# One-bank PSUM tiles after attention, GpSimd scaling of three blocks, and uneven row groups in an attention and feed-forward kernel

## The chip, the cores and the metric

The kernel runs on one core of one Trainium2 chip. The metric is the device time of one execution in microseconds (us); of several executions the median counts. Five engines of the core run their own instruction lists in order and wait for each other by semaphores: TensorE (PE, with its weight loads as PEld), VectorE (DVE), ScalarE (ACT), GpSimd (POOL) and SyncE (SP), which here issues nearly all DMA transfers.

## What is computed

Attention of 4 batches, 8 heads, 768 positions and head width 64, in which a query sees the 8 first keys and its 96 last ones, with a bias that falls with the distance; then a feed-forward layer of width 2048 with a sigmoid gate on the 3072 resulting rows:

```python
scores = scale * q @ k.T + bias                  # per batch and head
scores = where(is_global | is_local, scores, -1e9)
a = exp(scores - max(scores)); a = a / (sum(a) + 1e-09)
x = (a @ v) as 3072 rows of 512
h = x @ w_in                                     # 512 -> 2048
out = (h / (1 + exp(-h))) @ w_out                # 2048 -> 512
```

## The kernel before

**Blocks.** Attention is done in 24 blocks of 128 rows. For a block, PE turns K and Q into the layout it needs (`turn`, L626, copied out by ACT at L634) and multiplies them (`scores`, L659) into the four-bank PSUM tile `four`. DVE adds the bias and finds the maxima (`top_of`, L669, eight instructions), ACT takes the exponentials with their sums (`expo`, L677, eight instructions of 128x136), DVE inverts the sums (`guard`, `inverse`, L681 and L685), ACT multiplies by them (`norm`, L689, eight instructions), DVE transposes the result in two halves (`turn_p`, L703), and PE multiplies it with V (`values`, L722), into `four` again. `x_high` (ACT, L731) and `x_low` (DVE, L734) split the block's result into two parts for the first layer. GpSimd does small copies: the keys that a block shares with the one before (`carry`, L648 and L650) and the columns of the 8 first keys (`aside`, L694).

**First layer.** Blocks are collected in groups of row tiles (`GS`, eight groups of three). For each group and each of 16 slices f of w_in, `moe_h` (L819) issues 12 matmuls, which take the group's rows as columns (3 x 128 = 384), into one bank. ACT takes a tanh from it (L825), DVE multiplies (L829), and a DMA puts the result into DRAM (`moe_put`, L834). w_in arrives as raw 64-bit numbers, 1 MB at a time (`ws`, L431), and is turned into two float parts by three DVE instructions (L439, L445, L451), an ACT cast (L457) and a DVE subtraction (L461).

**Second layer.** Rows are taken in 12 pairs of row tiles. Each pair needs seven products (`product`, L876) of 24 matmuls with 256 columns, from sums and differences of quarters that are read back from DRAM. For a product ACT casts (`split_hi`, L866) and DVE subtracts (`split_lo`, L870); for some, DVE first adds quarters (`sums`, L856). Three buffers hold split inputs (`hl`). Each product is summed in one PSUM bank. It is then evicted by ACT (`keep_half`, L890) or DVE (`add_half`, L893) into the output tile. Beside that, DVE checks the number formats of all weights (L552, L558) and of V (L606), and at the end gathers the verdict (L1014 to L1081), by which a branch decides on a general version.

**Banks.** There are eight PSUM banks: four tiles of one bank each (`bank0` to `bank3`) and `four`, which is one tile of four banks. In the second layer a product takes any free bank of the eight; banks 4 to 7 are slices of `four`:

```python
four = psum.tile([P, 4, 512], F32, name="four")
banks = [psum.tile([P, 512], F32, name=f"bank{i}") for i in range(4)] + [four[:, i] for i in range(4)]
```

**Order.** A planner (`Plan.run`) goes through all operations with assumed costs and latencies and ranks from the table `PAR`, and writes each engine's list in the order in which it would have started them. Where its PE has nothing to do before the first layer, it puts in a matmul without use (`filler`, L1103). The recording layer derives waits from which tiles an instruction reads and writes.

Of the kernel before, what the change touches and what calls it, by code (L numbers as in the profile page):

```python
# [10 lines left out]
F32 = mybir.dt.float32  # L11
# [8 lines left out]
PSUM = bass.MemoryType.PSUM  # L20

P = 128
# [3 lines left out]
NR = 4  # L26
CH = Q + 2
WIN = NR * CH
# [9 lines left out]
    CAP=dict(po=6, h=4, tp=2), CST=dict(t=480, s=1000, top=220, exp=395, sc=300, tp=597, o=1500, o0=800, g=330),  # L38

    C0=17.5, CR=1.05, LW=14, LB=5.5, QB=3.5, RN=-1.8, RP=1.4, RV=2.0, RB=1.5, VL=1.5, SP=0, TE='ACT', KS=66, KE=203, KD=10000.0, KV=14990,  # L40

    BP=(4, 2), CF=8, AHEAD=9, GS=(3,) * 8, BD=(1, 0), EQ=4, B1R=-0.5, Q1=450, Q2=2400, CD=9, CS=3, SQ=((0, 0, 8), (1, 0, 8)), PB=4, AQ=4, O0=10.0, ON=11, PF=23,
# [147 lines left out]
def attn_moe(ctx, tc, q, k, v, n_global, n_local, w_in, w_out, out):  # L190
# [43 lines left out]
    four = psum.tile([P, 4, 512], F32, name="four")  # L234
# [166 lines left out]
    o_bias = steps(bias_own, [70, 200, 597, 597, 597], -4, [o, o_far], [*bt, tb])  # L401
    o_bias1 = steps(bias_prev, [570, 80, 80], PAR['B1R'], [o_bias], bt)
    o_b = {}
    for a in range(2):
        for first in (True, False):
            dve = bias_eng(first, a) is nc.vector
            o_b[first, a] = op(
                "DVE" if dve else "ACT", 597 if dve else 560, 2 * a - 0.5 if first else PAR["RB"] + 2 * a,
                (lambda first=first, a=a: bias_of(first, a)), [o_bias if first else o_bias1], bt,
            )  # L410
# [105 lines left out]
    def open_late():  # L516
        attn.close()
        st["late"] = ctx.enter_context(tc.tile_pool(name="late", bufs=1))
# [168 lines left out]
    def norm(i, a, c):  # L687
        x, m = blk[i]["p", a][:, c], a * NR + c
        nc.scalar.mul(x, x, blk[i]["S"][:, m:m + 1])  # L689
# [54 lines left out]
    for i in range(B * NJ):  # L744
# [43 lines left out]
        for n in ((0, 1),) if not PAR["SP"] else ((0,), (1,)):  # L788
# [4 lines left out]
            for a in n:  # L793
                o_y = [op("ACT", CST["sc"], r, (lambda i=i, a=a, c=c: norm(i, a, c)), [o], [pes_[a]]) for c in range(NR)]
                if j:
                    o_f.append(op("POOL", 150, r, (lambda i=i, a=a: aside(i, a)), o_y + o_n[-2:-1], [pes_[a], gs]))
                o_t.append(op("DVE", CST["tp"], r, (lambda i=i, a=a: turn_p(i, a)), o_y, [pes_[a], pts[a]]))
# [134 lines left out]
    for g in range(NPAIR):  # L932
# [9 lines left out]
        for m, (src, c) in enumerate(PROD):  # L942
# [19 lines left out]
            for p in range(HF):  # L962
                o = op("PE", 355, r, (lambda g=g, m=m, p=p, po=po: product(g, m, p, po)),
                       [hi, lo, *o_w2[p], o], [hl, po])
                if not g and not m and not p:
                    o["hold"] = 2
            o_p.append(o)
# [315 lines left out]
```

## Time and profile before

| | us |
|---|---|
| median of 3 runs | 669.76 (668.48 to 670.19) |
| the profiled execution | 672.28 |
| its span, first to last instruction | 670.5 |
| mean granted TensorE clock | 0.993 |
| busy: PE, DVE, ACT, POOL | 641.5, 514.6, 351.0, 32.7 |

The profile is of one execution, which took 2.5 us more than the median. Busy times are sums over the span; matmuls overlap, so the spacing of their starts says more than their durations. "Idle before" at a row is the time in which the engine waited just ahead of it, with the instruction that ended the wait; "issue" stands for idle time that no wait explains.

### The profile page before, as it was taken

The numbers are of one execution on the slowest core, as the hardware profiler recorded it, in microseconds if no ns is written. First come the engines' busy times: TensorE is split into PE (matmuls) and PEld (weight loads), VectorE is DVE, ScalarE is ACT, GpSimd is POOL, SyncE is SP. The second block draws the span as 40 slices with busy tenths as digits, with TensorE's granted clock in tenths as the row PEclk, the third lists the DMA queues.
The fourth block names the chain that finished last, engine by engine and source line by source line (L and its number), as shares of the span: only waits on it lengthen the run. The fifth ranks groups of instructions, "written<-read, shape, count | busy, mean of one in ns | idle before, by whom it ended". The sixth has DMA issues, their size and how long they took to land. (4 is left out here: it accounts for less than half of the span.)

```text
span 670.5 us, 20175 instructions
## 1 busy us (share of the span) xinstructions
PE 641.5 (96%) x8308; PEld 608.5 (91%) x8308; DVE 514.6 (77%) x1132; ACT 351.0 (52%) x915; POOL 32.7 (5%) x127
## 2 busy tenths in 40 slices
PE   8979989999999999999999999999999999999996
PEld 6859879999999999999999998988998999999996
DVE  5777886868845445467457989988998889999995
ACT  5958872598648556579454433333333333333431
POOL 4111100001000000010000000000000000000000
PEclk9989999999999999999999999999999999999999
DMA  7974997647645456653546788576658556656321
GB/s 123 232 218 109 289 225 223 183 119 192 167 113 124 109 145 165 167 137 82 136 115 205 239 237 282 189 224 215 198 161 255 180 181 190 208 191 218 106 80 35
DMA packets 180372, 116.83 MB, mean 174 GB/s; under 512 B 105396, under 2 KB 162996, under 8 KB 180276
## 3 DMA queue, kind: packets, MB, share of 16 engines
q1 hardware_dynamic: 179602, 115.24, 61.5%
q8 instruction: 66, 1.08, 0.7%
q10 hardware_dynamic: 674, 0.26, 0.1%
q14 instruction: 30, 0.25, 0.1%
HBM read 84.02 MB, written 31.46 MB: 172 GB/s over the span
## 5 line engine op out<-in xcount | busy, mean ns | idle before, releaser
L819 PE MATMUL bank<-xh,wi 128*128 128x384 f32 x1024 | 279.2, 344 | 0.0
L819 PEld LDWEIGHTS bank<-xh,wi 128*128 128x128 f32 x1024 | 187.7, 189 | 6.0 <-issue 5.3
L819 PE MATMUL bank<-xl,wi 128*128 128x384 f32 x512 | 173.2, 338 | 0.0
L876 PE MATMUL four<-wo,g 128*128 128x256 f32 x1035 | 133.1, 284 | 13.2 <-DVE o L893 9.8
L876 PEld LDWEIGHTS four<-wo,g 128*128 128x128 f32 x1035 | 125.8, 189 | 18.3 <-DVE o L893 13.5
L829 DVE SCALAR_TENSOR_TENSOR th<-th,bank 128x384 f32<-128x384 f32 x128 | 70.6, 552 | 69.2 <-ACT th L825 66.4
L825 ACT ACTIVATE th<-bank 128x384 f32<-128x384 f32 x128 | 62.6, 489 | 103.2 <-PE bank L819 101.8
L876 PE MATMUL bank<-wo,g 128*128 128x256 f32 x945 | 116.2, 282 | 0.0
L876 PEld LDWEIGHTS bank<-wo,g 128*128 128x128 f32 x945 | 113.8, 189 | 0.0
L819 PEld LDWEIGHTS bank<-xl,wi 128*128 128x128 f32 x512 | 97.0, 189 | 0.0
L866 ACT CAST g<-S 128x1024 fp32r<-128x1024 f32 x48 | 50.0, 1049 | 66.3 <-DVE S L856 34.9
L677 ACT ACTIVATE pe<-pe,NM 128x136 f32<-128x136 f32 x192 | 75.9, 399 | 5.9 <-DVE NM L669 5.8
L689 ACT ACTIVATE pe<-pe,S 128x136 f32<-128x136 f32 x192 | 61.8, 399 | 2.4 <-DVE S L685 2.4
L870 DVE TENSOR_TENSOR g<-S,g 128x1024 fp32r<-128x1024 f32 x48 | 58.4, 1219 | 2.3 <-ACT g L866 2.1
L866 ACT CAST g<-a 128x1024 fp32r<-128x1024 f32 x36 | 37.7, 1048 | 41.7 <-PE four L876 21.7
L669 DVE CUSTOM_DVE_ANT_0 pe<-four,B 128x136 f32<-128x136 f32 x192 | 45.2, 292 | 14.1 <-PE four L659 12.6
L870 DVE TENSOR_TENSOR g<-a,g 128x1024 fp32r<-128x1024 f32 x36 | 43.9, 1220 | 2.6 <-ACT g L866 2.5
L558 DVE TENSOR_REDUCE TOP<-c 128x1 f32<-128x512 int16 x64 | 43.0, 678 | 1.0 <-DMA c<-in_moe_w_in_dram 1.0
L703 DVE STREAM_TRANSPOSE pt<-pe 128x512 f32<-128x512 f32 x48 | 34.0, 708 | 12.3 <-ACT pe L689 12.2
L722 PEld LDWEIGHTS four<-pt,vt 32*64 32x64 f32 x2496 | 33.3, 130 | 5.8 <-issue 5.0
L677 ACT ACTIVATION_READ_ACCUMULATOR pe<-pe,NM 128x1 f32 x192 | 36.6, 191 | 0.0
L722 PE MATMUL four<-pt,vt 32*64 32x96 f32 (+3 forms) x2496 | 36.0, 243 | 0.0
(128 smaller groups left out, 575.2 us busy)
## 6 DMA issues: line engine op xcount, KB each, us to landing
gate<-th SPq DMA_DIRECT2D x128, 192.0 KB
a<-gate SPq DMA_DIRECT2D x48, 512.0 KB
ws<-in_moe_w_in_dram SPq DMA_DIRECT2D x8, 1024.0 KB
w<-in_moe_w_out_dram SPq DMA_DIRECT2D x16, 512.0 KB
c<-in_moe_w_in_dram SPq DMA_DIRECT2D x16, 512.0 KB
c<-in_moe_w_out_dram SPq DMA_DIRECT2D x16, 512.0 KB
vt<-in_v_dram SPq DMA_DIRECT2D x64, 96.0 KB
va<-in_v_dram SPq DMA_DIRECT2D x24, 256.0 KB
```

Source lines behind the costliest of these rows:

```text
L558: nc.vector.tensor_reduce(TOP[:, i, n:n + 1], top, AX.X, (ALU.min, ALU.max)[i], apply_absolute_value=True)
L669: nc.vector.tensor_tensor_reduce(blk[i]["p", a][:, c], four[:, c // 2 * 2 + a, c % 2 * WIN:(c % 2 + 1) * WIN], (B1 if i % NJ else B0)[:, a ...
L677: nc.scalar.activation(x, x, AF.Exp, bias=NM[:, n:n + 1], scale=-1.0, accum_out=blk[i]["S"][:, m:m + 1])
L689: nc.scalar.mul(x, x, blk[i]["S"][:, m:m + 1])
L703: nc.vector.transpose(y[:, :NR * NR * Q].rearrange("p (a r q) -> p a r q", a=NR, q=Q), x[:, :, :, :Q])
L722: nc.tensor.matmul(o, x, y, start=w == line[0], stop=w == line[-1])
L819: nc.tensor.matmul(ph, w1[f // 2][:, w, c, f % 2 * P:(f % 2 + 1) * P], x[:, c, :SIZE[g] * P], start=not c and not n, stop=c == NCC - 1 and ...
L825: nc.scalar.activation(th, mo["ph", g, f], AF.Tanh, scale=0.5)
L829: nc.vector.scalar_tensor_tensor(gf, gf, 1.0, mo["ph", g, f], ALU.add, ALU.mult)
L866: nc.scalar.copy(x[:, 0], mo["a", g, PROD[m][0]])
L870: nc.vector.tensor_sub(x[:, 1], mo["a", g, PROD[m][0]], x[:, 0].bitcast(F32))
L876: nc.tensor.matmul(y, a[:, i, p], w2[p, w, c], start=not p and not n, stop=p == HF - 1 and n == 2,)
```

## The change

When attention has ended (`open_late`), the four-bank tile is given back, and four one-bank tiles take its place, so that every product of the second layer lies in a tile of its own. The first matmul of the second layer is now put behind that point. For the first three blocks (`NB=3`) GpSimd multiplies by the inverted sums, in two instructions of 128x544 for a block instead of eight on ACT. The sums are inverted for each half by itself (`SP=1`). The first layer's groups have 3, 3, 2, 4, 4, 4, 4 row tiles. Some twenty numbers of the planner's table differ.

```diff
-    C0=17.5, CR=1.05, LW=14, LB=5.5, QB=3.5, ..., SP=0, TE='ACT', KS=66, KE=203, ...
+    C0=19.2, CR=1.35, LW=15, LB=3, QB=4.5, ..., SP=1, TE='ACT', NB=3, KS=64, KE=187, ...
-    BP=(4, 2), CF=8, AHEAD=9, GS=(3,) * 8, BD=(1, 0), ...
+    BP=(4, 2), CF=8, AHEAD=27, GS=(3, 3, 2, 4, 4, 4, 4), BD=(2, 1), ...
...
-    four = psum.tile([P, 4, 512], F32, name="four")
+    early = ExitStack()
+    ctx.enter_context(early)
+    four = early.enter_context(tc.tile_pool(name="four", bufs=1, space=PSUM)).tile([P, 4, 512], F32, name="four")
...
     def open_late():
         attn.close()
+        early.close()
+        x = ctx.enter_context(tc.tile_pool(name="last", bufs=1, space=PSUM))
+        banks[4:] = [x.tile([P, 512], F32, name=f"bank{i}") for i in range(4, 8)]
...
     def norm(i, a, c):
-        x, m = blk[i]["p", a][:, c], a * NR + c
-        nc.scalar.mul(x, x, blk[i]["S"][:, m:m + 1])
+        if c is None:
+            x = blk[i]["p", a]
+            y = blk[i]["S"][:, a * NR:(a + 1) * NR].unsqueeze(2).to_broadcast([P, NR, WIN])
+            nc.gpsimd.tensor_mul(x, x, y)
+        else:
+            x, m = blk[i]["p", a][:, c], a * NR + c
+            nc.scalar.mul(x, x, blk[i]["S"][:, m:m + 1])
...
+                if i < PAR["NB"]:
+                    o_y = [op("POOL", CST["scp"], r, (lambda i=i, a=a: norm(i, a, None)), [o], [pes_[a]])]
...
                     o["hold"] = 2
+                    plan.after(o, o_late)
```

PE in the second layer before, where a product in `four` ends and the next one in `four` begins (g is the split input, wo the weights, and the wait names the engine whose semaphore is waited for):

```order
L876 MATMUL four<-wo_0_6289,g_5_7332 128x256
L876 MATMUL four<-wo_1998,g_6_7371 128x256 [waits Activation_49]
L876 MATMUL four<-wo_1998,g_6_7371 128x256
L876 MATMUL four<-wo_1998,g_6_7371 128x256 [waits DVE_49]
L876 MATMUL four<-wo_2656,g_6_7371 128x256 x3
L876 MATMUL four<-wo_2977,g_6_7371 128x256 [waits DVE_49]
L876 MATMUL four<-wo_2977,g_6_7371 128x256 x2
```

The same place after:

```order
L889 MATMUL bank_5565<-wo_1984,g_6_7350 128x256 [waits Activation_49]
L889 MATMUL bank_5565<-wo_1984,g_6_7350 128x256
L889 MATMUL bank_5565<-wo_1984,g_6_7350 128x256 [waits DVE_49]
L889 MATMUL bank_5565<-wo_2264,g_6_7350 128x256 x3
L889 MATMUL bank_5565<-wo_2906,g_6_7350 128x256 x3
```

The first two waits, for the two parts of the split input, are in both; the third, for a DVE eviction that reads another bank of `four`, is gone. Before, 26 matmuls of the second layer wait for a DVE eviction and 9 for an ACT eviction of the tile `four`; after, none does.

ACT before, around the scaling of blocks 1 and 2 (pe is a half of a block's scores):

```order
L689 ACTIVATE pe_79<-pe_79,S 128x136 x4
L689 ACTIVATE pe_80<-pe_80,S 128x136 x4
L677 ACTIVATE pe_77,S<-pe_77,NM 128x136 x3
L634 COPY QT<-bank_91 128x512
L677 ACTIVATE pe_78,S<-pe_78,NM 128x136 x4
L731 CAST xh<-four 128x4x128
L457 CAST wi_704<-ws_465 128x1024
L689 ACTIVATE pe_77<-pe_77,S 128x136 x4
L689 ACTIVATE pe_78<-pe_78,S 128x136 x4
```

POOL after, for the same two blocks:

```order
L696 TENSOR_TENSOR pe_79<-pe_79,S 128x544
L704 COPY pgr_104<-pe_79 128x4x8
L655 COPY KT<-KT 128x4x4x2
L653 COPY KT<-KT 128x4x102
L696 TENSOR_TENSOR pe_80<-pe_80,S 128x544
L704 COPY pgr_104<-pe_80 128x4x8
L655 COPY KT<-KT 128x4x4x2
L653 COPY KT<-KT 128x4x102
L696 TENSOR_TENSOR pe_77<-pe_77,S 128x544
L704 COPY pgr_103<-pe_77 128x4x8
L696 TENSOR_TENSOR pe_78<-pe_78,S 128x544
```

The sixteen scalings of these blocks left ACT's list, and four multiplications entered POOL's, between the copies of keys that the next block's scores wait for. On PE, 200 fillers became 173: ahead of the first matmul of the first layer there stand 191 before and 173 after.

SP before, where the loads of K and Q for later blocks (kn, qn), the last raw w_in parts (ws), V (vt) and stores of the first layer (gate) stand in a row:

```order
L431 DMA ws_1462<-in_moe_w_in_dram 128x4x512
L834 DMA gate_1033<-th 384x1x128
L587 DMA kn<-in_k_dram 128x8x64
L587 DMA qn<-in_q_dram 128x8x64
L594 DMA vt<-in_v_dram 32x12x64 x8
L834 DMA gate_1033<-th 384x1x128
L587 DMA kn<-in_k_dram 128x8x64
L834 DMA gate_1712<-th 384x1x128
L431 DMA ws_1721<-in_moe_w_in_dram 128x4x512
```

SP after, there:

```order
L592 DMA kn<-in_k_dram 128x8x64
L592 DMA qn<-in_q_dram 128x8x64
L847 DMA gate_1070<-th 384x1x128
L599 DMA vt<-in_v_dram 32x12x64 x8
L847 DMA gate_1070<-th 384x1x128
L433 DMA ws_1617<-in_moe_w_in_dram 128x4x512
L433 DMA ws_1679<-in_moe_w_in_dram 128x4x512
L847 DMA gate_1710<-th 384x1x128 x2
L592 DMA kn<-in_k_dram 128x8x64
```

One pair of K and Q moved ahead of the last two ws loads, and the K load behind V now stands behind both of them.

## Rows read from the trace of the kernel before

**Rows 1.** Busy time by stage (core: us, engines busy (x instructions), PEclk, DMA share, GB/s)

```profile
0.00:50.20 50.20, 42.94 (x884) 34.80 (x885) 32.33 (x115) 35.04 (x118) 11.95 (x54) 0.97 0.87 191
50.20:405.10 354.90, 351.53 (x5400) 332.42 (x5399) 245.00 (x699) 223.12 (x691) 20.80 (x73) 1.00 0.63 166
405.10:665.70 260.60, 246.82 (x2026) 241.16 (x2024) 236.37 (x319) 92.88 (x107) 0.00 (x0) 1.00 0.58 184
```

**Rows 2.** Waits of PE in the second layer: us in total, times, longest

```profile
PE four L876 <- DVE o L893: 9.8, 18, 1.0
PE four L876 <- ACT E L890: 1.4, 3, 0.5
PE four L876 <- ACT o L890: 1.4, 3, 0.5
```

**Rows 3.** Timeline of PE in the second layer: start, us, instruction, xcount [idle before]

```profile
418.81 8.35 PE L876 MATMUL bank<-wo,g 128*128 128x256 f32 x69
...
437.28 1.67 PE L876 MATMUL four<-wo,g 128*128 128x256 f32 x12 [0.52 <-DVE o L893]
439.47 1.33 PE L876 MATMUL four<-wo,g 128*128 128x256 f32 x9 [0.52 <-DVE o L893]
...
501.69 5.86 PE L876 MATMUL bank<-wo,g 128*128 128x256 f32 x48
```

**Rows 4.** Waits of DVE in the second layer

```profile
DVE o L893 <- PE four L876: 14.2, 22, 1.1
DVE g L870 <- ACT g L866: 4.7, 11, 0.7
...
DVE o L893 <- PE bank L876: 1.6, 4, 0.6
DVE TOP L558 <- DMA c<-in_moe_w_in_dram: 1.0, 2, 0.7
```

**Rows 5.** Timeline of DVE around the fifth product of a pair

```profile
501.89 0.42 DVE L893 SCALAR_TENSOR_TENSOR o<-four,o 128x256 f32<-128x256 f32 x1 [0.79 <-PE four L876]
502.24 1.22 DVE L870 TENSOR_TENSOR g<-S,g 128x1024 fp32r<-128x1024 f32 x1
503.37 0.42 DVE L893 SCALAR_TENSOR_TENSOR o<-bank,o 128x256 f32<-128x256 f32 x1
```

**Rows 6.** Timeline of PE at the end of the first layer

```profile
403.96 0.51 PE L819 MATMUL bank<-xh,wi 128*128 128x384 f32 x2
...
404.48 0.51 PE L819 MATMUL bank<-xh,wi 128*128 128x384 f32 x2
```

**Rows 7.** Timeline of PE ahead of the first layer: fillers, and scores with their stops

```profile
31.32 2.14 PE L1103 MATMUL bank<-wx 128*128 128x256 bf16 x18
...
36.63 1.16 PE L659 MATMUL four<-KT,QT 64*32 64x136 f32 x32 [2.55 <-issue]
...
48.92 0.53 PE L659 MATMUL four<-KT,QT 64*32 64x136 f32 x17 [1.83 <-issue]
...
50.27 0.67 PE L819 MATMUL bank<-xh,wi 128*128 128x384 f32 x1
```

**Rows 8.** Timeline of ACT, POOL and DVE ahead of the first layer

```profile
32.88 2.50 ACT L689 ACTIVATE pe<-pe,S 128x136 f32<-128x136 f32 x8
...
40.87 0.52 POOL L648 COPY KT<-KT 128x408 f32<-128x408 f32 x1 [2.67 <-DVE NM L669]
...
46.82 1.22 DVE L445 SCALAR_TENSOR_TENSOR ws<-ws 128x1024 uint32<-128x1024 uint32 x1
...
47.55 0.56 POOL L694 COPY pgr<-pe 128x32 f32<-128x32 f32 x1 [6.15 <-ACT pe L689]
48.81 0.21 POOL L694 COPY pgr<-pe 128x32 f32<-128x32 f32 x1 [0.70 <-ACT pe L689]
```

**Rows 9.** Timeline of PE where K and Q are waited for

```profile
86.19 0.63 PE L626 MATMUL bank<-ident,kn 128*128 128x128 f32 x4 [1.86 <-DMA kn<-in_k_dram]
...
88.63 0.63 PE L626 MATMUL bank<-ident,qn 128*128 128x128 f32 x4 [0.76 <-DMA qn<-in_q_dram]
```

More of the change, by code (lines that the diff above doesn't have):

```diff
@@ L36 @@
     LAT=140, SD=125, DL=2100, DV=2300, DW=2900, DB=3500, DS=3500, DO=3400, MG=60, T2=45000, LAT2=230, MG2=400, F0=600, F1=1200, C1=400, C2=1650, COLD=4400, WEND=60000,
-    CAP=dict(po=6, h=4, tp=2), CST=dict(t=480, s=1000, top=220, exp=395, sc=300, tp=597, o=1500, o0=800, g=330),
-    C0=17.5, CR=1.05, LW=14, LB=5.5, QB=3.5, RN=-1.8, RP=1.4, RV=2.0, RB=1.5, VL=1.5, SP=0, TE='ACT', KS=66, KE=203, KD=10000.0, KV=14990,
-    BP=(4, 2), CF=8, AHEAD=9, GS=(3,) * 8, BD=(1, 0), EQ=4, B1R=-0.5, Q1=450, Q2=2400, CD=9, CS=3, SQ=((0, 0, 8), (1, 0, 8)), PB=4, AQ=4, O0=10.0, ON=11, PF=23,
+    CAP=dict(po=6, h=4, tp=2), CST=dict(t=435, s=1220, top=220, exp=393, sc=300, scp=1150, tp=610, o=1880, o0=1050, g=330),
+    C0=19.2, CR=1.35, LW=15, LB=3, QB=4.5, RN=3, RP=-0.4, RV=2.4, RB=8.5, VL=0.0, SP=1, TE='ACT', NB=3, KS=64, KE=187, KD=10000.0, KV=11530,
+    BP=(4, 2), CF=8, AHEAD=27, GS=(3, 3, 2, 4, 4, 4, 4), BD=(2, 1), EQ=4, B1R=-4.0, Q1=450, Q2=2400, CD=9, CS=3, SQ=((0, 0, 8), (1, 0, 8)), PB=4, AQ=4, O0=5.0, ON=15.0, PF=24,
 )
@@ L400, in attn_moe @@
     o = op("PE", 120, -99, (lambda tp=tb: spread_par(tp)), [o], [tb])
-    o_bias = steps(bias_own, [70, 200, 597, 597, 597], -4, [o, o_far], [*bt, tb])
-    o_bias1 = steps(bias_prev, [570, 80, 80], PAR['B1R'], [o_bias], bt)
+    o_bias = steps(bias_own, [190, 300, 762, 821, 821], -4, [o, o_far], [*bt, tb])
+    o_bias1 = steps(bias_prev, [701, 273, 550], PAR['B1R'], [o_bias], bt)
     o_b = {}
@@ L407, in attn_moe @@
             o_b[first, a] = op(
-                "DVE" if dve else "ACT", 597 if dve else 560, 2 * a - 0.5 if first else PAR["RB"] + 2 * a,
+                "DVE" if dve else "ACT", 530 if dve else 646, 2 * a - 0.5 if first else PAR["RB"] + 2 * a,
                 (lambda first=first, a=a: bias_of(first, a)), [o_bias if first else o_bias1], bt,
@@ L793, in attn_moe @@
             for a in n:
-                o_y = [op("ACT", CST["sc"], r, (lambda i=i, a=a, c=c: norm(i, a, c)), [o], [pes_[a]]) for c in range(NR)]
+                if i < PAR["NB"]:
+                    o_y = [op("POOL", CST["scp"], r, (lambda i=i, a=a: norm(i, a, None)), [o], [pes_[a]])]
+                else:
+                    o_y = [op("ACT", CST["sc"], r, (lambda i=i, a=a, c=c: norm(i, a, c)), [o], [pes_[a]]) for c in range(NR)]
                 if j:
```

## Prediction

> **What bounds the kernel now.** I read the busy times by stage first [rows 1]. They cut the span at the first matmul of the first layer (50.2 us), at the first of the second layer (405.1) and at its last (665.7). In the middle stage PE is busy for 351.5 of 354.9 us, so nothing but PE's own work sets its length. In the last stage PE is busy for 246.8 of 260.6 us and DVE for 236.4: both are close to being the bound. In the first stage no engine is full (PE 42.9, ACT 35.0, DVE 32.3 of 50.2 us); there a chain of waits sets the time, and a good part of PE's work is fillers.
>
> Next come the waits of PE in the second layer [rows 2]: 18 times for a DVE eviction (9.8 us) and 6 times for an ACT one (2.8 us), always for a product that was about to be computed in another bank of `four`. The idle time of 0.52 us is not the whole price of such a stop, and the timeline shows what is [rows 3]. In a run without stops, 69 matmuls start within 8.07 us (8.35 less the last one's 0.28), which is 0.1187 us from start to start. The run of 12 that begins at 437.28 starts its last matmul at 438.67, and the next begins at 439.47: 0.80 us instead of 0.12, and the first matmuls behind a stop are slower too (9 take 1.33 us, without a stop it would be 8 x 0.1187 + 0.28 = 1.23). So a stop costs about 0.8 us. From the other side: 2016 matmuls by 0.1187 are 239.3 us, the stage took 260.6, so 21.3 us are lost; some 0.7 of it is the few matmuls of the checks, and the rest over 25 stops (the 24 of the rows, and one of the kind at the end for the verdict) is 0.8 us again.
>
> **The change, part by part.** *One-bank tiles.* The lists show that none of the second layer's matmuls waits for an eviction of its neighbour's bank any more. That takes 24 stops by 0.8 us, 19.2 us, off PE. What is late next is DVE. It has 236.4 us of work in that stage [rows 1], and the change takes only a last piece of weight preparation out of it (0.7 us), against 239.3 us of PE. Its waits are of two kinds [rows 4]. It waits 15.8 us for products that it is to evict: that is DVE being ahead, and this shrinks as PE gets faster. It waits 4.7 us for ACT casts and 1.0 us for transfers, and these may stay. How much room there is shows at the fifth product of a pair, the tightest one [rows 5]: DVE waits 0.79 us for a product to end, evicts it from 501.89, subtracts from 502.24 and is done at 503.46. PE runs on without a stop [rows 3]: its product begins 24 matmuls after 501.69, at 504.54, and needs the subtracted part with its third matmul, at 504.78. That is 1.3 us of slack, and for these five products DVE kept pace with an unstopped PE. A pair takes PE 168 x 0.1187 = 19.9 us, and DVE on average 236 / 12 = 19.7. A pair with more checks than average, or a late ACT cast, therefore eats the slack. I allow 2 us for stops of that new kind (floor 0, and up to 9 by the rival below): 19.2 - 2 = 17.2 us gained.
>
> *Uneven row groups.* Three matmuls of 384 columns take 0.52 us [rows 6], 0.1735 each; one of 256 columns takes 0.1187 [rows 3]. The line through both gives 0.2283 for 512 columns. 1536 x 0.1735 = 266.5 us become 384 x 0.1735 + 768 x 0.2283 + 192 x 0.1187 = 264.7: a gain of 1.8 us. No row shows 512 columns; in proportion to the columns (0.2313) the gain would be -0.5, and the line's is nearer, since it is drawn through two rows. I take 1.5. The ACT and DVE work of the wider pieces is the same number of elements in fewer instructions, and in the middle stage it lies under PE (ACT 223, DVE 245 of 355 us).
>
> *GpSimd scaling and the start.* ACT loses 24 instructions ahead of the first layer; eight take 2.50 us [rows 8], so 7.5 us of its 35.0. The last block of a chain then no longer waits for eight scalings but for one GpSimd multiplication of its half. None is in the trace: a copy of 408 elements takes 0.52 us there [rows 8], so 544 elements with one input would be 0.70, and twice that, 1.4, with two inputs; I take 1.2, nearer to the upper one since both operands are read. Six of them cost GpSimd 7.2 us of a stage in which it idles for 38. What waits behind them there are the key copies for the next block's scores; since the multiplications are released by other blocks' exponentials, I cost that at nothing, and if the cover is gone at 1.2 us for each of three blocks. What PE gets of all this is read from its list: 27 fillers fewer at 0.109 us ((2.14 - 0.28) / 17 [rows 7]), 2.9 us. PE stops twice on scores for 2.55 and 1.83 us without a wait that the profile shows [rows 7]; I leave them as they are, as the same loads are queued around them. If they vanished as well, the stage would be 4.4 us shorter; if the shorter list only means longer stops, nothing is gained.
>
> *Loads.* Behind 50 us, PE waited 1.86 and 0.76 us for K and Q [rows 9], while weights were loading. In the new list one K and Q pair goes ahead of the last two weight parts, the next one behind both. I expect one place relieved and one made worse: 0, with 3 us to the good (all those waits) and 4 to the bad (a megabyte more to pass before K).
>
> *The end.* The verdict's last instructions move behind the last product on DVE: 0.5 us lost (0 to 2).
>
> *Sum.* 672.3 (the profiled execution: 670.5 of span and 1.8 around it) - 17.2 - 1.5 - 2.9 - 0 + 0.5 = 651.2 us. That execution is 2.5 us above the median of the runs, 669.76, so for a median I say 648.7.
>
> **A rule against the change.** A small GpSimd copy took 0.56 us at 47.55, and 0.21 at 48.81 [rows 8]; the long one ended just when a DVE instruction with two inputs in SBUF did (46.82 + 1.22 = 48.04). The Trainium skill, SBUF - State Buffer, section Who interferes with whom, says that such a DVE instruction and a GpSimd one that reads SBUF exclude each other for the whole instruction; the trace agrees for the copy. The Trainium skill, GPSIMD Engine Reference, section 3.1, measures 4497 ns for a two-input operation of 2048 elements, by which an estimate for 544 is 1.2 us; no run here shows it. By that figure the sum would be the same.
>
> **The rivals.** *DVE takes PE's place in the second layer.* If DVE's waits for ACT and transfers stay (5.7 us) and half of those for products do (7.9), the stage lasts 235.7 + 13.6 = 249.3 us, a gain of 11.3 instead of 17.2: 654.6. For it: DVE's 236 us against 239. Against it: the slack of 1.3 us that comes back in each pair.
>
> *GpSimd and DVE hold each other up.* The six multiplications fall among DVE's two-input weight instructions of 1.2 us each. If each holds DVE, or is held, for its whole time, that is 7.2 us in a stage in which DVE idles for 18; with half of it on the chain, the start loses 3.6 and the 2.9 is not gained: 655.2. That is the rule of the SBUF page above, at its price by the rows.
>
> *Everything falls well.* PE at its floor in the second layer (2.0 more), the two stops at the start gone (4.4), K and Q in time (2.6): 639.7.
>
> *K and Q late for all that follows: slower.* The table's shorter lead for loads (`LB` from 5.5 to 3) could leave each block waiting as at 86 us, 2.6 us for a block. From nine of the some 18 blocks after the first layer's start on, that eats the 21 us; at 12 blocks it gives 648.7 + 31.2 = 680. Against it: PE is idle for only 3.4 us of the whole middle stage [rows 1], of which the two waits at 86 and 88 us are 2.6, and DMA there has a mean share of 0.63, so that loads have room later on.
>
> *It does not do what it says.* If stops of the same size come back at the same places, because the evictions are needed for another reason, what is left is 669.8 - 3.9 = 665.9. The waits are gone from the list, so this is unlikely.
>
> **How the numbers follow.** Forecast 0.55; DVE as the bound 0.22; GpSimd and DVE 0.07; everything well 0.09; K and Q late 0.04; no effect on the stops 0.03. The forecast's own spread is 644 to 653. The range reaches to the two rivals at 655 and partly to the one at 640: 642 to 657. Faster than before by over 0.3%, about what a measurement of this kernel can tell from no change, is every case but the late loads: 0.95; slower 0.04; the same 0.01.
>
> **What would show it.** In the profile after, the waits of PE for L893 and L890 of before must be gone in the second layer; if PE then waits for the subtraction (L870), above all at a pair's fifth product, DVE is the bound, and the stage is near 249 us instead of 243. The first layer's 512-column matmuls should be 0.228 us apart. The first of them all should come at about 47 us. A GpSimd multiplication far above 1.4 us, or DVE instructions of 2 us beside it, would show the rival at the start. The prediction is wrong if the second layer is not at least 10 us shorter, or if the middle stage is longer than before.

## The result, and the profile after

The changed kernel takes 650.8 us (median of 4 runs, 645.2 to 653.7) against 670.0 for the kernel before in the same session: a ratio of 0.970, with a 95% interval of 0.9625 to 0.978. The forecast was 648.7, with a range of 642 to 657. A second set of runs gave 651.0 (645.3 to 653.0), ratio 0.9727 (0.9702 to 0.9752). The profiled execution of after took 653.09 us, 2.3 more than the median; its span is 651.3. By stage (start, first layer, second layer, tail; columns as in [rows 1]):

```profile
0.00:49.20 49.20, 40.97 (x863) 32.88 (x864) 35.39 (x129) 27.13 (x92) 19.03 (x60) 0.97 0.86 195
49.20:407.37 358.17, 350.77 (x5204) 296.50 (x5203) 245.66 (x721) 218.55 (x674) 22.09 (x73) 1.00 0.63 165
407.37:647.46 240.09, 240.09 (x2025) 239.87 (x2023) 233.12 (x315) 92.83 (x107) 0.00 (x0) 1.00 0.62 199
647.46:651.30 3.84, 0.31 (x5) 0.10 (x4) 0.96 (x3) 0.00 (x0) 0.00 (x0) 1.00 0.15 47
```

Against [rows 1] the second layer is 20.5 us shorter (260.6 to 240.1), the start 1.0 and the tail 1.0 (4.8 to 3.8), and the stage of the first layer is 3.3 us longer. That is the 19.2 us between the two profiled executions, and the second layer alone is more than all of it.

In the second layer PE is busy for 240.09 of 240.09 us. None of the waits of [rows 2] is left, nor any other, and the first run there is unbroken over six products, with (17.83 - 0.28) / 147 = 0.1194 us from start to start:

```profile
407.37 17.83 PE L889 MATMUL bank<-wo,g 128*128 128x256 f32 x148
```

DVE is what changed places with it. Its waits there, which answer to [rows 4]:

```profile
DVE o L906 <- PE bank L889: 2.7, 5, 1.0
DVE g L883 <- ACT g L879: 2.5, 4, 1.5
```

It waited 15.8 us for products before and 2.7 now, 4.7 us for casts before and 2.5 now: most of the 24 us in which DVE was idle before was time in which it was ahead of a stopped PE. 7 us are left.

The start and the first layer went less well. Every row of PE's timeline with an idle time of over 1 us between 2 us and the end of the first layer:

```profile
35.58 0.45 PE L664 MATMUL four<-KT,QT 64*32 64x136 f32 x11 [3.42 <-issue]
48.96 0.49 PE L631 MATMUL bank<-ident,qn 128*128 128x128 f32 x3 [2.32 <-issue]
72.08 0.66 PE L631 MATMUL bank<-ident,kn 128*128 128x128 f32 x4 [1.30 <-DMA kn<-in_k_dram]
79.86 0.69 PE L631 MATMUL bank<-ident,kn 128*128 128x128 f32 x4 [1.04 <-DMA kn<-in_k_dram]
...
96.30 0.63 PE L631 MATMUL bank<-ident,kn 128*128 128x128 f32 x4 [1.24 <-DMA kn<-in_k_dram]
...
161.36 0.39 PE L832 MATMUL bank<-xl,wi 128*128 128x256 f32 x1 [1.88 <-issue]
...
184.01 0.63 PE L631 MATMUL bank<-ident,qn 128*128 128x128 f32 x4 [1.51 <-DMA qn<-in_q_dram]
```

The four waits for K and Q come to 5.1 us. The two stops on the way to the first layer, which answer to [rows 7], grew from 4.4 to 5.7 us. And the matmuls of 512 columns, in the first layer's last groups:

```profile
371.90 0.39 PE L832 MATMUL bank<-xl,wi 128*128 128x512 f32 x1
372.13 0.63 PE L832 MATMUL bank<-xh,wi 128*128 128x512 f32 x2
372.60 0.40 PE L832 MATMUL bank<-xl,wi 128*128 128x512 f32 x1
```

Three of them take 0.70 us, 0.2333 each, against 0.1735 for 384 columns [rows 6].

### The profile page after: what moved, and what is told of

It reads as the page before. It is cut to its first block, busy times and chain, and to the rows that moved or that the text cites. A ratio compares the mean times of both kernels' runs of the same rounds, so it can differ in the third digit from the quotient of the medians.

```text
span 651.3 us, 19662 instructions
## 1 busy us (share of the span) xinstructions
PE 632.1 (97%) x8089; PEld 569.3 (87%) x8089; DVE 515.1 (79%) x1166; ACT 338.5 (52%) x873; POOL 41.1 (6%) x133
## 5 line engine op out<-in xcount | busy, mean ns | idle before, releaser
L832 PE MATMUL bank<-xh,wi 128*128 128x512 f32 (+2 forms) x896 | 264.0, 368 | 0.0
L889 PE MATMUL bank<-wo,g 128*128 128x256 f32 x1980 | 237.2, 281 | 0.0
L889 PEld LDWEIGHTS bank<-wo,g 128*128 128x128 f32 x1980 | 235.9, 189 | 0.2
L832 PEld LDWEIGHTS bank<-xh,wi 128*128 128x128 f32 x896 | 163.2, 188 | 28.0 <-issue 5.4
L832 PE MATMUL bank<-xl,wi 128*128 128x512 f32 (+2 forms) x448 | 162.3, 362 | 1.9 <-issue 1.9
L842 DVE SCALAR_TENSOR_TENSOR th<-th,bank 128x512 f32<-128x512 f32 (+2 forms) x112 | 68.0, 608 | 69.8 <-ACT th L838 69.1
L838 ACT ACTIVATE th<-bank 128x512 f32<-128x512 f32 (+2 forms) x112 | 60.0, 535 | 112.9 <-PE bank L832 109.9
L832 PEld LDWEIGHTS bank<-xl,wi 128*128 128x128 f32 x448 | 84.2, 188 | 12.6 <-issue 2.3
L674 DVE CUSTOM_DVE_ANT_0 pe<-four,B 128x136 f32<-128x136 f32 x192 | 46.1, 291 | 18.3 <-PE four L664 18.0
L664 PE MATMUL four<-KT,QT 64*32 64x136 f32 x1536 | 29.4, 280 | 3.7 <-issue 3.4
L664 PEld LDWEIGHTS four<-KT,QT 64*32 64x32 f32 x1536 | 22.1, 105 | 10.7 <-issue 9.2
```

The lines of the kernel that those rows point to most:

```text
L664: nc.tensor.matmul(o, t["QT"][r, g, Q * c:Q * (c + 1)], t["KT"][r, g, c:c + NR], start=True, stop=True)
L674: nc.vector.tensor_tensor_reduce(blk[i]["p", a][:, c], four[:, c // 2 * 2 + a, c % 2 * WIN:(c % 2 + 1) * WIN], (B1 if i % NJ else B0)[:, a ...
L832: nc.tensor.matmul(ph, w1[f // 2][:, w, c, f % 2 * P:(f % 2 + 1) * P], x[:, c, :SIZE[g] * P], start=not c and not n, stop=c == NCC - 1 and ...
L838: nc.scalar.activation(th, mo["ph", g, f], AF.Tanh, scale=0.5)
L842: nc.vector.scalar_tensor_tensor(gf, gf, 1.0, mo["ph", g, f], ALU.add, ALU.mult)
L889: nc.tensor.matmul(y, a[:, i, p], w2[p, w, c], start=not p and not n, stop=p == HF - 1 and n == 2,)
```

## The experiments

Each kernel was timed beside the kernel before, on the same chip as that. They did not all run on one chip, so small differences between kernels are read from the ratios. "First" is the start of the first layer, "layer 1" and "layer 2" the lengths of the two stages in the kernel's profiled execution, as they are cut above.

| kernel | median us | ratio to before (95%) | first | layer 1 | layer 2 |
|---|---|---|---|---|---|
| before | 669.5 to 670.0 | | 50.2 | 354.9 | 260.6 |
| after | 650.8 | 0.9702 (0.9625 to 0.9780) | 49.2 | 358.2 | 240.1 |
| after, again | 651.0 | 0.9727 (0.9702 to 0.9752) | 42.8 | 356.7 | 240.1 |
| four_kept | 675.0 | 1.0055 (1.0027 to 1.0084) | 49.6 | 357.5 | 263.6 |
| split_only | 651.8 | 0.9733 (0.9689 to 0.9778) | 49.5 | 352.0 | 242.4 |
| dve_more12 | 659.6 | 0.9850 (0.9804 to 0.9896) | 43.1 | 356.4 | 249.5 |
| shift64 | 650.5 | 0.9707 (0.9662 to 0.9752) | 46.1 | 357.0 | 241.6 |
| long_fillers | 648.9 | 0.9693 (0.9663 to 0.9724) | 43.0 | 357.0 | 240.1 |
| split_scale | 652.6 | 0.9728 (0.9699 to 0.9757) | 48.1 | 353.4 | 246.2 |
| act_scales | 648.2 | 0.9665 (0.9642 to 0.9688) | 47.0 | 356.9 | 240.2 |
| groups_of_3 | 656.2 | 0.9794 (0.9772 to 0.9817) | 47.7 | 356.1 | 243.9 |
| early_loads | 652.9 | 0.9730 (0.9706 to 0.9753) | 48.2 | 358.3 | 241.4 |
| gp_3to5 | 647.7 | 0.9683 (0.9652 to 0.9714) | 46.7 | 353.7 | 241.3 |
| gp_3to8 | 646.3 | 0.9655 (0.9629 to 0.9681) | 46.3 | 354.8 | 240.1 |

### Is it the tile? four_kept and split_only

```diff
 # four_kept: the kernel after
     def open_late():
         attn.close()
-        early.close()
-        x = ctx.enter_context(tc.tile_pool(name="last", bufs=1, space=PSUM))
-        banks[4:] = [x.tile([P, 512], F32, name=f"bank{i}") for i in range(4, 8)]
```

> The kernel after with one part undone: the four-bank tile stays to the end, so the products of the second layer lie in its slices again. All orders are those of after. If the tile was the cause of the stops, they come back, some 24 to 26 of about 0.8 us, the second layer takes 259 to 262 us instead of 240, and the time is 651 + 20 = 671 us (667 to 675). Rival: the second layer became shorter because the table's new numbers ordered its DVE and ACT work better; then the stage stays under 250 us and the time under 661.

It took 675.0 us, 24 more than after and even 0.55% more than before. The stops are back, and the shape is that of [rows 2] and [rows 3]:

```profile
407.10:670.70 263.60, 247.71 (x2025) 241.32 (x2023) 236.08 (x316) 92.94 (x107) 0.00 (x0) 1.00 0.55 181
```

```profile
PE four L886 <- DVE o L903: 10.4, 20, 0.6
PE four L886 <- ACT E L900: 2.4, 5, 0.5
PE four L886 <- ACT o L900: 1.9, 4, 0.5
PE four L886 <- DVE CS L1022: 0.9, 1, 0.9
PE four L886 <- DVE RV L1033: 0.3, 1, 0.3
```

29 stops behind evictions instead of 24, two more behind weight checks, and a stage 23.5 us longer than after's: 0.76 us for each of the 31, or 0.81 if the evictions' 29 are made to pay for all of it. The prediction had 0.8 from before's rows.

```diff
 # split_only: the kernel before, with the edit above put in, and
                     o["hold"] = 2
+                    plan.after(o, o_late)
```

> The kernel before with this part alone: one-bank tiles when attention ends, and the first product put behind that point. Everything else, its table and its groups, is as before. If the tile is the whole cause, the second layer falls from 260.6 to 240 us and the time from 670 to about 649.5 (647 to 653). Rival: DVE, which has 236.4 us of work there, becomes the bound: the stage is near 249 us with PE waiting for the subtraction (L870 of before) and the time near 658.

651.8 us: this part by itself gives 17.7 us, about as much as the whole change. The second layer lasts 242.4 us, and PE waits only twice:

```profile
PE bank L1014 <- DMA c<-in_moe_w_out_dram: 0.9, 1, 0.9
PE bank L881 <- DVE g L875: 0.8, 1, 0.8
```

One is for the load of a weight check and one for a subtraction. The rival of 249 us is out. What else was changed is worth about 1 us in all, within the spread of the runs; that this is a sum of gains and losses is seen below.

### How near is DVE? dve_more12

```diff
 # the kernel after, in split_lo
         nc.vector.tensor_sub(x[:, 1], mo["a", g, PROD[m][0]], x[:, 0].bitcast(F32))
+        if m == 0:
+            nc.vector.tensor_sub(x[:, 1], mo["a", g, PROD[m][0]], x[:, 0].bitcast(F32))
```

> The kernel after, with the subtraction of the first product of each of the 12 pairs written twice, so DVE has 12 x 1.14 = 13.6 us more to do in the second layer; nothing else differs. DVE was busy for 233.1 of 240.1 us there, so 7 us were free. If DVE is close behind PE, as the prediction's second case has it, the free 7 us are used up and the stage lasts 233.1 + 13.6 = 246.7 us and up to 4 more for waits that stay: 247 to 251, and the time is 658 to 662. Rival: DVE's place in time leaves no use for the free time, since each doubled instruction stands right ahead of a product that waits for it; then each pair loses close to the whole 1.14 us, the stage lasts 253 to 254 and the time is about 664. If PE does not feel it, 651.

```profile
399.53:649.04 249.51, 243.55 (x2025) 240.47 (x2023) 244.62 (x326) 91.56 (x107) 0.00 (x0) 1.00 0.59 192
```

```profile
PE bank L891 <- DVE g L883: 5.0, 7, 1.2
PE bank L891 <- DVE g L885: 0.8, 2, 0.6
```

The first of the 12 repeats ran ahead of the stage, at 371 us, so DVE has 11.5 us more to do in it (busy for 244.6 instead of 233.1). Of these 9.4 come out as time (240.1 to 249.5), and only 2.1 fit into the 7 us in which DVE was idle. Seven of the nine stops (5.0 of 5.8 us) are not behind the repeated subtraction but 98 matmuls into a pair, at the third matmul of its fifth product, as in these rows:

```profile
564.17 11.79 PE L891 MATMUL bank<-wo,g 128*128 128x256 f32 x98
577.11 8.19 PE L891 MATMUL bank<-wo,g 128*128 128x256 f32 x67 [1.16 <-DVE g L883]
```

That is the place that the prediction named as the tightest. So it is DVE's work as a whole that holds PE up, and not only that a longer instruction stands right ahead of a product: DVE is then the bound, as in the prediction's second case. That case was near, with some 1% of DVE's work (2.1 of 233 us) between it and the forecast, but it was not the case of this kernel. The profiled execution was the fastest of the four, 4.9 us under their median.

### What are PE's stops at the start? after again, shift64 and long_fillers

In the trace of after, 64 transfers on a queue of kind "instruction" go with 8089 weight loads and as many matmuls of PE, 253 of them a piece.

```profile
PE 632.1 (97%) x8089; PEld 569.3 (87%) x8089; DVE 515.1 (79%) x1166; ACT 338.5 (52%) x873; POOL 41.1 (6%) x133
...
q8 instruction: 64, 1.05, 0.7%
```

The two stops at the start come at the 613th and the 870th record of PE's weight loads, the few waits between the loads counted as records too (without them, the 606th and the 862nd load; where a text here says "613th load", the record is meant). The two places are about twice 128 records apart. The records of the queue show a packet of 16 KB from 32.99 to 34.30 us, 1.28 us ahead of the restart at 35.58, and one from 46.44 to 47.40, 1.56 us ahead of the restart at 48.96. In before the stops of [rows 7] lie at the 614th and 870th record, with packets that end at 35.17 and 47.43 us, 1.46 and 1.49 us ahead of the restarts. One of the packets, by the queues' sums in the stretch from 32.95 to 34.35 us of after:

```profile
q1 hardware_dynamic: 499, 0.29, 104.7%
q8 instruction: 1, 0.02, 5.8%
```

The packets of the other transfers add up to all of the DMA engines' time there. This suggests that PE waits for its own instructions: a piece would hold 128 loads with their matmuls, which last 22 us in the first layer (128 x 0.175), but only about 4 us from the 485th record at 28.2 us to the first stop, where scores and values of attention stand close together. The test moves the same work to another place in the stream:

```diff
 # shift64: the kernel after, in filler
-        nc.tensor.matmul(bank(b)[:, c:c + 2 * P], warm[:, :P], warm, start=True, stop=True)
+        st["n"] = st.get("n", 0) + 1
+        for h in (0, P) if st["n"] <= 64 else ():
+            nc.tensor.matmul(bank(b)[:, c + h:c + h + P], warm[:, :P], warm[:, :P], start=True, stop=True)
+        if st["n"] > 64:
+            nc.tensor.matmul(bank(b)[:, c:c + 2 * P], warm[:, :P], warm, start=True, stop=True)
```

> The kernel after, with each of PE's first 64 fillers written as two matmuls of half the columns, so that all that follows stands 64 weight loads and matmuls later in PE's instruction stream while PE's work is the same in time. In after, PE stopped for 3.42 us ahead of the 54th of the 64 score matmuls at 35.6 us and for 2.32 ahead of the second matmul of a turn of Q at 49.0, at the 613th and 869th weight load of its stream, and an instruction transfer of 16 KB ended 1.3 and 1.6 us before each of the two restarts. If the stops are PE's instructions coming late, they stay at the 613th and 869th load and so come 64 loads earlier in the work (in the values of block 1 at about 28 us and ahead of the scores of block 3), and the sum of both is 3 to 9 us: time 651 (647 to 656). If they belong to the scores and the turn (a wait that the profile does not show), they stay at the 54th score matmul and at the turn, at the 677th and 933rd load, with the same time.

```profile
29.19 0.72 PE L1121 MATMUL bank<-wx 128*128 128x256 bf16 x5
33.22 2.50 PE L1121 MATMUL bank<-wx 128*128 128x256 bf16 x11 [3.32 <-issue]
35.66 1.39 PE L664 MATMUL four<-KT,QT 64*32 64x136 f32 x64
```

The stop is again ahead of the 613th load, which is now a filler: a matmul that needs nothing. The packet here ends at 31.63 us, 1.59 us ahead of the restart. The 64 scores that were cut in two in after run through. At the 870th load there is no stop in this execution; the second packet behind the one above, the piece in question if the order is that of after, had ended at 42.79 us, and PE came there at 44.56. So the stops belong to the place in the stream and not to the work. The expectation that both stops come back was half wrong: whether a piece is late differs from one execution to the next. Why a piece is late is argued from the full DMA engines and was not tried. The same kernel run again shows how much the stops differ:

> The kernel after once more, unchanged, beside the kernels of the same call, since its first runs spread from 645.2 to 653.7 us. If the spread is the stops at the start, which take 0.7 us in one trace of this order and 5.7 in another, the runs spread by 5 us or more again, and the profiled execution's own time is explained by the start of its first layer: span = start + 357 + 240 + 4, each within 2 us. Against the kernel with ACT's scalings and the same table (648.2 us): if GpSimd's scaling is worth the 2.9 us of the prediction, after is faster than that, under 646; if it is worth nothing or less, 649 to 653.

```profile
33.04 0.45 PE L664 MATMUL four<-KT,QT 64*32 64x136 f32 x11 [1.50 <-issue]
```

This execution (645.27 us) had only this stop at the start, at the same matmul, and the first layer began at 42.8 us instead of 49.2. Two more kernels have the same PE list up to the second layer, and four executions of it can be compared: stops of "issue" of 5.7, 5.4, 1.5 and 0.7 us in all (after, four_kept, after again, dve_more12) go with a first layer at 49.2, 49.6, 42.8 and 43.1.

The stops explain 4.2 of the 6.4 us between the two executions of after. Most of the rest is PE's clock, by the stretches of the first profile of after:

```profile
31.00:34.00 3.00, 1.16 (x54) 0.84 (x53) 3.00 (x4) 0.32 (x1) 2.18 (x2) 1.00 1.22 257
34.00:36.00 2.00, 0.42 (x12) 0.21 (x13) 0.27 (x1) 0.00 (x0) 0.00 (x0) 1.00 1.01 350
36.00:38.00 2.00, 2.00 (x19) 1.57 (x16) 1.90 (x17) 0.50 (x2) 0.21 (x1) 0.75 0.92 253
38.00:40.00 2.00, 2.00 (x11) 1.67 (x10) 1.78 (x2) 0.51 (x2) 0.00 (x0) 0.50 0.06 16
40.00:42.00 2.00, 2.00 (x52) 1.62 (x53) 0.00 (x0) 1.59 (x7) 0.53 (x1) 0.90 0.58 131
```

Cut finer where the clock falls and rises:

```profile
36.50:37.00 0.50, 0.50 (x7) 0.44 (x6) 0.50 (x7) 0.50 (x2) 0.00 (x0) 0.99 1.20 316
37.00:37.50 0.50, 0.50 (x5) 0.35 (x3) 0.50 (x7) 0.00 (x1) 0.00 (x0) 0.50 1.13 253
...
40.00:40.50 0.50, 0.50 (x5) 0.35 (x4) 0.00 (x0) 0.50 (x4) 0.36 (x1) 0.60 0.00 0
40.50:41.00 0.50, 0.50 (x7) 0.50 (x5) 0.00 (x0) 0.36 (x2) 0.17 (x1) 1.00 0.43 102
```

Behind the stop of 3.42 us the granted clock (third column from the right) falls to 0.50, the lower level of 1.2 GHz, and the finer cut shows it there from 37.0 to 40.4 us. PE is busy all that time, so 3.4 us at half the clock cost it 1.7 (an estimate from these rows); some 0.5 of the 6.4 us stay open. In the second execution, with its stop of 1.50 us, it stays at 1.00:

```profile
34.00:36.00 2.00, 2.00 (x21) 1.84 (x19) 2.00 (x18) 0.68 (x3) 0.00 (x0) 1.00 0.77 139
36.00:38.00 2.00, 2.00 (x72) 1.73 (x76) 1.57 (x2) 2.00 (x9) 1.52 (x1) 1.00 1.04 389
```

The ten timed runs of after agree with this: the two fastest, 645.2 and 645.3 us, have a mean granted clock of 1.000 and 0.999, the others, at 648.5 to 653.7, one of 0.994 to 0.997. It is not the whole of their spread, since runs of 648.5 and 653.1 us both have 0.997.

The Trainium skill, Runtime: NRT & Kernel Launch, section Instruction fetch mechanics, says that instructions come in blocks of 16 KiB, 256 of them, by a DMA queue of the sequencer's own, and that this is mostly hidden. The size and the queue agree with the 64 packets here. That it is hidden holds in the second layer, where PE never stopped, and not at the start, with stops of up to 3.42 us.

```diff
 # long_fillers: the kernel after, in filler and in the list of clean halves beside it
-    clean = [(b, c) for b in range(8) for c in (0, 2 * P)]
+    clean = [(b, c) for b in range(8) for c in (0, 0)]
...
-        nc.tensor.matmul(bank(b)[:, c:c + 2 * P], warm[:, :P], warm, start=True, stop=True)
+        st["n"] = st.get("n", 0) + 1
+        if st["n"] % 2:
+            nc.tensor.matmul(bank(b)[:, :4 * P], warm[:, :P], warm.unsqueeze(1).to_broadcast([P, 2, 2 * P]), start=True, stop=True)
```

> The kernel after, with each two fillers of 256 columns made one of 512, so that PE's work ahead of the first layer is the same in time and 86 weight loads and matmuls fewer in number. If the stops at the start are PE's instructions coming late, they are again only at places 128 loads apart (the 613th, the 741st, the 869th load of its stream), which is now other work; the same attention work falls into fewer instruction transfers, but each has less time, so the sum of stops stays at 3 to 8 us and the time at 651 within 3. If the stops belong to the scores of block 2 and the turn of Q, they stay ahead of the same matmuls as in after.

648.9 us, with an interval that overlaps after's. In the profiled execution the stops of "issue" are 0.22, 1.42 and 1.72 us, the last ahead of the 2543rd record, where after's last one (1.88 us) is ahead of the 2799th, 256 records further; at the start nothing longer than 0.22 is left. That agrees with the stream's places, but with intervals that overlap it stays open whether fewer and longer fillers make the start better.

### The scaling by GpSimd: split_scale and act_scales

```diff
 # split_scale: the kernel after with the planner's table of before, but
-    SP=0, TE='ACT', KS=66,
+    SP=1, TE='ACT', NB=3, KS=66,
 # act_scales: the kernel after, but
-    SP=1, TE='ACT', NB=3, KS=64,
+    SP=1, TE='ACT', NB=0, KS=64,
```

> The table and groups of before, with the one-bank tiles and with the GpSimd scaling of three blocks and its halves (NB=3, SP=1), so that against the kernel with the one-bank tiles alone (651.8 us, first layer from 49.5 us) the scaling is tried by itself. If the scaling shortens the chain at the start by 2.9 us as predicted, the first layer begins at 46 to 47 us and the time is about 649. Rival: the start follows the arrival of PE's instructions, so it lies between 43 and 50 us whatever the scaling does, and the time is 652 within 2. Third: GpSimd and DVE hold each other up and the start is later than 50, time above 653.

652.6 against split_only's 651.8: the scaling gives nothing that can be measured. Its second layer took 246.2 us in the profile, 3.8 more than split_only's, with PE waiting 2.1 us for the load of a check and 1.9 for a subtraction; since the scaling ends long before, this is a matter of how that execution's loads and DVE work fell.

> The kernel after with all blocks scaled by ACT (NB=0), ordered anew by the planner with the rest of after's table. If the GpSimd scaling gives what the prediction said, the first layer starts 2 to 3 us later than after's 49.2 us, at 51 to 52, and the time is 653 to 654. Rival: the start is set by when PE's instructions arrive, and the shorter chain only turns into a longer stop; then the start lies in the same spread as other runs of after's order (43 to 50 us so far) and the time is 651 within 2.

648.2 us, ratio 0.9665 (0.9642 to 0.9688), and after measured with as many runs 0.9727 (0.9702 to 0.9752): without the scaling by GpSimd the kernel is faster, by 0.6%. In the profile of act_scales PE has no stop of "issue" at all ahead of the first layer. Its list has 208 fillers where after's has 173, and they lie between the bursts of attention. That these give the instructions time to arrive is argued: the planner ordered the rest anew too, and the number of fillers alone does not settle it, since before has 200 and stopped for 4.4 us, and after's list stopped for between 0.7 and 5.7 us in four executions. After begins the first layer 4.2 us earlier than act_scales (42.8 against 47.0) in the execution with the one short stop, and 2.2 us later in the one with both stops; that the second was so in eight of the ten runs is suggested by their clocks, and no profile shows it.

### Groups and loads: groups_of_3 and early_loads

```diff
 # groups_of_3: the kernel after, but
-    GS=(3, 3, 2, 4, 4, 4, 4),
+    GS=(3,) * 8,
 # early_loads: the kernel after, but
-    LW=15, LB=3,
+    LW=15, LB=5.5,
```

> The kernel after with the groups of row tiles as before, eight groups of three, and the rest of its table; the planner orders the work anew. In the trace of after, matmuls of the first layer start 0.2330 us apart with 512 columns, 0.1759 with 384 and 0.1175 with 256, so that 768, 384 and 192 of them take 269.0 us, where 1536 of 384 at 0.1756 took 269.7 before: the width is worth 0.7 us. By this the stage of the first layer is 358 to 359 us and the time within 2 us of after, 651. The prediction put the width at 1.5 us, the time at 652.3. Rival: the uneven groups, or what they do to the order, cost the 3.2 us by which after's middle stage is longer than before's; then the stage is near 355 and the time near 648.

Neither: 656.2 us, 5 more than after. The stage of the first layer is 2 us shorter than in after's first execution, as the rival has it, but only 0.6 shorter than in its second (356.1 against 356.7), so the uneven groups are not shown to cost anything there. The second layer is 3.8 us longer:

```profile
PE bank L1022 <- DMA c<-in_moe_w_out_dram: 1.6, 1, 1.6
PE bank L889 <- DVE g L883: 1.2, 2, 0.8
```

The profiled execution was the fastest of its five runs, 2.8 us under their median, so these rows do not show all that the kernel loses. The planner orders the weight checks anew with the groups; which of its choices costs the rest stays open.

> The kernel after with the lead of K, Q and V loads as before (LB=5.5 instead of 3). In after's first layer PE waited 5.1 us for K and Q, in before 2.9. If the shorter lead is the cause, the waits fall by 2 to 4 us, the middle stage from 358.2 to some 355, and the time to about 648. Rival: the loads ahead of them on the same queue, weights above all, set when K and Q arrive; then the waits stay at 4 to 5 us or move elsewhere, and the time is 651 within 2.

652.9 us: nothing gained. The waits for K and Q are 2.4 us against after's 5.1. But with the same PE list and the short lead they are 4.2 us in after's second execution, 2.6 in four_kept and 1.7 in dve_more12, with 1.1 to 1.7 us more behind ACT at one of the same places. So one execution of early_loads does not show that the lead is their cause. Stops of "issue" of 2.24 and 1.82 us stand at 74 and 80 us, each 1.4 to 1.5 us behind the end of an instruction packet, and the stage is as long as after's (358.3). So behind 50 us too a piece of instructions can be the next thing to be late.

### A faster version: gp_3to5 and gp_3to8

```diff
 # gp_3to8: the kernel after, but (gp_3to5: with blocks 3, 4, 5)
-    NB=3,
+    NB=(3, 4, 5, 6, 7, 8),
-                if i < PAR["NB"]:
+                if i in PAR["NB"]:
```

> The kernel after with GpSimd scaling blocks 3 to 5 instead of 0 to 2; the planner orders the work anew. With ACT scaling all blocks PE waited once for 3.7 us at 63.5 us, where ACT was busy with scalings of these blocks, and had no stop at the start, because more fillers lay between the bursts of attention. If both hold, the start has few stops and the wait of 3.7 us goes: 644 to 647 us. Rival: what is gained at that place is lost at the next load of K or to a longer stop for instructions: 648 within 2.

> As the kernel that scales blocks 3 to 5 on GpSimd, but blocks 3 to 8. If ACT's scalings still delay PE behind block 5, this is 1 to 2 us faster than that one; if PE sets the time there, the two are the same within 2 us, at 645 to 649.

In act_scales PE waits once at 67 us behind ACT's scalings:

```profile
67.25 0.63 PE L631 MATMUL bank<-ident,kn 128*128 128x128 f32 x4 [3.71 <-ACT pe L699]
```

With GpSimd scaling these blocks the row is gone; in gp_3to8 a wait of 1.7 us for Q stands near its place, at 66.6 us. The kernels take 647.7 and 646.3 us. The second has the ratio 0.9655 (0.9629 to 0.9681), beside after's 0.9727 (0.9702 to 0.9752) in the same set of runs, so it beats after by 0.7%. Against act_scales the gain, 1.9 us, is within the intervals. How much of it is the scaling and how much the new order, which left gp_3to8 without a stop at the start, was not tried apart.

## Why the prediction was right, and where not

**One-bank tiles: right, and a little too cautious.** Forecast 19.2 us for 24 stops of 0.8, less 2 for new stops behind DVE, 17.2. The trace of after shows 20.5, this part alone 17.7 (and 18.2 in its stage), and its undoing 24. The price of a stop, 0.8 us instead of the 0.5 that the waits show, is what four_kept measured again (0.76 to 0.81). The allowance of 2 us was not needed in after, where PE has no wait at all in the second layer, and about needed in split_only (1.7 us).

**DVE as the bound: rightly the smaller case.** The condition of that rival was that DVE's other waits stay. They did not: those for casts went from 4.7 to 2.5 us and those for products from 15.8 to 2.7, where the rival left 7.9. dve_more12 shows the rival's mechanism at work as soon as DVE has 5% more to do (11.5 of 233 us), and at the fifth product, where the prediction looked for it.

**Column widths: the step was wrong.** The line was drawn through 384 columns in the first layer and 256 in the second. The row above gives 0.2333 us for 512, near the value in proportion (0.2313) and not on the line (0.2283). Over all unbroken runs of the first layer the medians from start to start are 0.117, 0.175 and 0.234 us for 256, 384 and 512 columns, in proportion to the columns. The width is then worth nothing (1536 x 0.175 = 268.8 us before, 269.4 after), and 0.7 by the means that the expectation of groups_of_3 gives; not 1.5. There is hardly a fixed part in a matmul to be saved. The line's two points came from two layers (256 columns take 0.1187 in the second, 0.117 in the first), and the point at 384 from three matmuls at 0.1735, which is under the median; both bend it the same way.

**The start: wrong for the median.** Each multiplication took 1.09 us, near the 1.2 taken, and the list did lose its 27 fillers. The step that failed is leaving the two stops "as they are", for the reason that the same loads are queued around them. They are pieces of PE's instructions that come late, and they change from one execution to the next: 5.7 and 5.4 us in two executions of this list, 1.5 and 0.7 in two others. In the first two the lower bound named there, that the shorter list only means longer stops, is what came (in after the first layer is 1.0 us earlier instead of 2.9). In the other two the first layer began at 42.8 and 43.1 us, which is close to 50.2 - 2.9 - 4.4 = 42.9, the fillers and both stops of before gone, though 1.5 us of stop were left in one of them. So the price of the fillers may hold where the stops allow it. For the median, act_scales, with ACT's scalings and the planner's other order, makes the sign of the term negative by some 3 us; that the fillers it has more are the reason is not shown.

**GpSimd and DVE: the lock is there, its price is small.** In these rows the multiplication at 17.92 holds a small DVE instruction that takes 0.16 us elsewhere, the one at 31.14 stretches a DVE subtraction of 1.22 us to 1.80, and that one in turn holds the copy at 32.30, else 0.21 us:

```profile
17.92 1.09 POOL L696 TENSOR_TENSOR pe<-pe,S 128x544 f32<-128x544 f32 x1 [1.32 <-DVE S L690]
...
31.14 1.09 POOL L696 TENSOR_TENSOR pe<-pe,S 128x544 f32<-128x544 f32 x1 [0.29 <-DVE S L690]
32.30 1.09 POOL L704 COPY pgr<-pe 128x32 f32<-128x32 f32 x1
```

```profile
18.11 0.93 DVE L686 TENSOR_SCALAR S<-S 128x4 f32<-128x4 f32 x1
...
31.52 1.80 DVE L463 TENSOR_TENSOR wi<-ws,wi 128x1024 fp32r<-128x1024 f32 x1
```

Held pairs end together (17.92 + 1.09 = 19.01 and 18.11 + 0.93 = 19.04; 31.52 + 1.80 = 33.32 and 32.30 + 1.09 = 33.39). The Trainium skill, SBUF - State Buffer, section Who interferes with whom, states such a lock for the whole instruction, and the trace agrees. The rival priced at 7.2 us for six multiplications did not come: DVE lost about 1.4 us at these two places.

**Loads: the balance was 2 us off.** K and Q cost 5.1 us of waits instead of [rows 9]'s 2.6 and some smaller ones, 2.9 in all. The forecast of 0 had 4 to the bad as its end. The waits differ between executions of the same list (4.2, 2.6 and 1.7 us in the three others, with more behind ACT), so how much of the 2 us belongs to the new order of the loads stays open; early_loads shows only that the longer lead does not pay.

**A sign that the prediction had set for itself.** It was to be wrong if the second layer is not at least 10 us shorter, or if the middle stage is longer than before. The second layer is 20.5 us shorter. The middle stage is longer, 358.2 us against 354.9, and from 356.4 to 357.5 in the three other executions of the list. So the prediction is right on the stage that carries the gain and wrong on the middle one, where it had PE's own work setting the length and 1.5 us gained: PE waited there for K and Q and, for 1.9 us at 161 us, for its instructions.

**The end: wrong sign, 1.5 us.** The verdict's last cast takes 0.13 us behind the last eviction and hides in the wait for the output's transfer; the tail became 1.0 us shorter instead of 0.5 longer. The transfer is issued 0.5 us behind the last product in both kernels, and all is over 3.3 us later instead of 4.4. The tail is 3.8 us in nearly all profiles with the table of after, but 6.8 in that of long_fillers, which ends alike; the cause was not tried.

**The sum.** Predicted -21.1 us between profiled executions, measured -19.2. The main term was 3.3 us too small, and the smaller ones were off by +2 each at the start and the loads and, in the first layer, by 0.8 or more and one new stop of 1.9 us; the end gave 1.5 back. The right total owes something to that balance; the range, which was built on the second layer, was right for its own reason.

## What to carry to other kernels

A tile that spans several PSUM banks ties its parts together in the program's waits, whatever the hardware could do: where products rotate through such slices, split the tile, and price a stop by the spacing of the matmuls around it and not by the idle time in the waits. Before calling an engine the next bound, look at what its idle time waits for: waits for the engine that gets faster vanish with it. And where PE's idle time is put down to "issue", look for the instruction queue's packets beside it: a burst of very short matmuls can outrun its own instructions, and what a shorter list gains can then be lost in longer stops.

## What the runs showed of the hardware that was not expected

- PE can run out of instructions. In before, after, four_kept, shift64 and the second execution of after it stopped ahead of the 613th or 614th record of its weight loads, whatever stood there, for 1.5 to 3.4 us, and went on 1.3 to 1.6 us after a 16 KB packet of the instruction queue had ended. In dve_more12, with the same list as after, the stops at the start came to 0.7 us.
- A stop of 3.42 us was followed by 3.4 us at a granted clock of 0.50, one of 1.50 us by none. Stops and clock together are about 5.9 of the 7.8 us between the two profiled executions of after, which run the same list; for its other runs this is only suggested by their mean clocks.
- A matmul of the first layer, with its own weight load, costs 0.457, 0.456 and 0.457 ns a column at 256, 384 and 512 columns (medians of 0.117, 0.175 and 0.234 us): wider ones save hardly anything.
